# Strassen's form for the values' projection of an attention block, over pairs of token tiles

## The chip, the core and the metric

The kernel runs on one core of a Trainium2 chip. The metric is the device time of one execution in microseconds (us). Engines: PE (TensorE, matmul), ACT (ScalarE), DVE (VectorE), POOL (GpSimd) and SP (SyncE, which here only issues DMAs).

## The reference

Everything is float32. S = 2048 tokens, D = 640 channels, H = 32 heads of 20 channels.

```python
g = sigmoid((x * gate_w).sum(-1, keepdims=True))
qkv = (x @ wqkv).reshape(B, S, 3, H, Dh).transpose(2, 0, 3, 1, 4)
q, k, v = qkv[0], qkv[1], qkv[2]
o = softmax(q @ k.T * Dh ** -0.5) @ v               # per head
a = o.transpose(0, 2, 1, 3).reshape(B, S, D) @ wo
u = gelu(einsum("bsd,sf->bdf", layernorm(x), w1) + b1)   # mixer: over the tokens
b = transpose(einsum("bdf,fs->bds", u, w2) + b2)
return g * a + (1 - g) * b
```

## The kernel before

A float32 product is made of three float32r products. Every operand is split into a high and a low part (`hi_lo`: ACT copies the high part, DVE or POOL subtracts for the low part), and `mm3` adds high·high, high·low and low·high in one PSUM bank.

The stages follow each other on PE: the first two of ten 128-column blocks of q and k (16 units of `qk_unit`, each 15 matmuls of 512 columns, to 63 us), the values (called V here, 63 to 134 us), the other 24 units of q and k (to 216 us), the mixer's two products (to about 720 us) with part of a score pass between them, the attention loop, and the output product. PE, ACT and DVE run in the order in which the code is written (`manual_schedule`); POOL and SP are ordered by the tile scheduler up to the end of V and by hand after it.

A unit's PSUM bank is one of four in turn (`one_tile`: s3, pv, one0, one1). After its matmuls ACT writes the high part (`evh`, three buffers), DVE the low part (`evl`, two buffers), and SP stores both to DRAM. For the second block of k every second unit also stores a difference of two units: DVE copies or subtracts (`kf`), ACT takes the high part (`dh`), DVE the low part in place, and POOL issues four stores (`kd_d`). A buffer is written again only after the store that reads it has landed.

V goes over two column halves (`half`, the first with two more columns, the gate's weights and ones) and 16 token tiles of 128. A tile is 15 matmuls: five channel blocks, three products each, with the x tile as weights and 322 or 320 columns of `wv` moving. ACT copies a tile into `vt` (two ACTIVATEs of 160 columns, L469), SP stores it to `v_d`. The two extra columns go to `gs`, and after the first half one DVE instruction makes `negm` (minus the mean of x). In the second half ACT has one more instruction for each tile: the square of x minus its mean, summed into `ssq` (`stats_unit`, tile `xn`, L444). The next stage's weights `w[2]` are split four tiles before V ends.

Of the kernel before, what the change touches and what calls it, by code (L numbers as in the profile page):

```python
# [31 lines left out]
def gated_mix(ctx, tc, xT, x, wqk, wv0, wv1, wo, w1, w1t, b1, w2, b2, out):  # L32
# [6 lines left out]
    def hi_lo(hi, lo, src, hi_eng=None, lo_eng=None):  # L39
        if hi_eng is nc.scalar:  # L40
            nc.scalar.activation(hi, src, AF.Copy)  # L41
        else:
            (hi_eng or nc.vector).tensor_copy(hi, src)
        (lo_eng or nc.vector).tensor_sub(lo, src, hi.bitcast(F32))  # L44
# [6 lines left out]
    def mm3(ps, pairs, between=lambda i: None):  # L51
        n = len(pairs)
        for i, (ah, al, bh, bl) in enumerate(pairs):
            for k, (a, b) in enumerate(((ah, bh), (ah, bl), (al, bh))):
                nc.tensor.matmul(ps, a, b, start=(i == 0 and k == 0), stop=(i == n - 1 and k == 2))  # L55
            between(i)
# [256 lines left out]
    def qk_unit(m, w, q):  # L313
        wh, wl = w
        ps = one_tile([P, 512], f"qk{m}_{q}")
        mm3(ps, [(wh[:, c], wl[:, c], xh[c][q], xl[c][q]) for c in range(NC)], *([keep_warm] if m == q == 0 else []))
# [24 lines left out]
        nc.vector.tensor_sub(kd, kd, ps)  # L341
# [6 lines left out]
        put(kd_d[0, rows, cols], dh.bitcast(F32))
        put(kd_d[1, rows, cols], kd)
# [61 lines left out]
    wvs = [[[pvp.tile([P, HALF + 2 * (1 - half)], F32R, name=f"wv{i}{half}_{c}") for c in range(NC)]
            for i in range(2)] for half in range(2)]
    wv_raw = {}

    def load_wv(half, c):
        n = HALF + 2 * (1 - half)
        raw = pvp.tile([P, HALF + 2], F32, tag="wvr", bufs=5, name=f"wvr{half}_{c}")
        nc.sync.dma_start(raw[:, :n], (wv1 if half else wv0)[:, c])
        wv_raw[half, c] = raw[:, :n]

    def split_wv(half, c):
        hi_lo(wvs[half][0][c], wvs[half][1][c], wv_raw.pop((half, c)), hi_eng=nc.scalar)

    for c in range(NC):
        load_wv(0, c)
    for n in range(8):
        if 2 <= n < 2 + NC:
            split_wv(0, n - 2)
            load_wv(1, n - 2)
# [4 lines left out]
    nc.gpsimd.dma_start(b2_t, b2)
    xjs = {}

    def stats_load(t):
        if t < NT:
            xjs[t] = pvp.tile([P, D], F32, tag="xn", bufs=4, name=f"xn{t}")
            nc.gpsimd.dma_start(xjs[t], x[t * P:(t + 1) * P, :])  # L440

    def stats_unit(t):
        c = slice(t, t + 1)
        nc.scalar.activation(xjs[t], xjs[t], AF.Square, bias=negm[:, c], accum_out=ssq[:, c])  # L444

    for half in range(2):
        wvh, wvl = wvs[half]
        width = HALF + 2 if half == 0 else HALF
        for t in range(NT):
            n = NT * half + t  # L450
            if n == NT - 2:
                for i in range(4):
                    stats_load(i)
            if n == NT:
                nc.vector.tensor_scalar_mul(negm, gs[:, :, 1], -1.0 / D)
            if n in (2, 4, 6, 8, 10):
                split_wv(1, n // 2 - 1)
            if n == 2 * NT - 8:
                raws[2] = w_dma(2)
            if n == 2 * NT - 4:  # L460
                w[2] = load_w(2, raws[2])
# [3 lines left out]
            vt = pvp.tile([P, 8, NPAIR], F32, tag="vt", bufs=3, name=f"vt{half}_{t}")  # L465
            nc.gpsimd.memset(vt[:, :, VW: 32], 0.0)
            for j in range(2):
                nc.gpsimd.memset(vt[:, :, 32 * j + DH], 1.0)
                nc.scalar.activation(vt[:, :, 32 * j: 32 * j + DH], ps[:, :HALF].rearrange("p (h j w) -> p h j w", j=2, w=DH)[:, :, j], AF.Copy)  # L469
            nc.sync.dma_start(v_d[half, t], vt.rearrange("p h w -> p (h w)"))  # L470
            if half == 0:
                nc.vector.tensor_copy(gs[:, t], ps[:, HALF:])
# [90 lines left out]
    for n, (m, q) in enumerate(units):  # L563
        if n % 4 < 2 and n // 4 * 4 + 4 < len(units):
            m2 = units[n // 4 * 4 + 4][0]
            if n % 4 == 0:
                raws[m2] = w_dma(m2)
            else:
                w[m2] = load_w(m2, raws[m2])
        if n == 8:  # L570
# [10 lines left out]
        last_stores = qk_unit(m, w[m], q)  # L581
# [675 lines left out]
```

## Time and profile before

| | us |
|---|---|
| median of three runs | 1765.78 (1764.94 to 1765.88) |
| profiled execution | 1765.93 |
| its span, first to last instruction | 1764.1 |
| q and k, first 16 units | to 63.06 |
| V | 63.06 to 133.9 |
| q and k, other 24 units | to 216.1 |

The span is 1.83 us shorter than the profiled execution's time. In the rows of the profile, "x480" is a count of instructions, a time in brackets is how long the engine sat idle before the row, and "<-" in the brackets names what ended that. A matmul's row of 0.3 us is the time until its result is out; the next matmul starts earlier, so the pace is read from the starts.

### The profile page before, as it was taken

To read this page: it belongs to the slowest core of one execution; us is meant where nothing else is said; L and a number is where in the kernel's file an instruction comes from. 1 tells how busy PE (TensorE), PEld (TensorE's weight loads), DVE (VectorE), ACT (ScalarE), POOL (GpSimd) and SP (SyncE) were. 2 spreads that over 40 slices of the span, in tenths; PEclk is the share of its full clock that TensorE was granted. 3 is DMA by queue.
4 is the path that set the end of the run, shared out by engine and by line. 5 is a ranking of instruction groups with operands and counts; after the bars stand their busy time and mean duration, and the time that the engine had idled before them with its cause. 6 is when DMAs were issued, how large, how long until landed. Compare 5 with 4: busy or idle time off the path is not lost.

```text
span 1764.1 us, 39591 instructions
## 1 busy us (share of the span) xinstructions
PE 1757.8 (100%) x15020; PEld 1089.8 (62%) x15020; DVE 1223.2 (69%) x2377; ACT 1481.9 (84%) x2565; POOL 665.5 (38%) x990
## 2 busy tenths in 40 slices
PE   9999999999999999999999999999999999999999
PEld 7998899999999999533333333333333333333379
DVE  6303289989999889776777676776777677767335
ACT  5354388888888886799999999999999999999941
POOL 1223577789877777211211111121322122111420
PEclk9999999999999999999999999999999999999999
DMA  8767876567675564334314224043263143301444
GB/s 304 248 194 252 268 182 172 143 179 206 181 191 147 164 177 145 88 78 113 65 28 94 55 60 98 19 98 83 43 147 65 33 102 76 73 20 45 141 155 173
DMA packets 156529, 225.20 MB, mean 128 GB/s; under 512 B 66620, under 2 KB 93644, under 8 KB 152912
## 3 DMA queue, kind: packets, MB, share of 16 engines
q1 hardware_dynamic: 137550, 192.81, 39.8%
q0 software_dynamic: 15568, 23.95, 5.8%
q10 hardware_dynamic: 3220, 5.90, 1.1%
q8 instruction: 118, 1.93, 0.5%
q14 instruction: 73, 0.60, 0.1%
HBM read 166.88 MB, written 55.36 MB: 126 GB/s over the span
## 4 chain that ended last, share of the span: by engine, by line
PE 99%; DMA 1%; ACT 0%; DVE 0%; issue 0%; SPq 0%; ACTq 0%; DVEq 0%
PE pv L936 29%; PE st L1035 22%; PE s L213 12%; PE y L49 10%; PE u L49 10%; PE qk L55 8%; PE v L55 4%; PE a L1155 1%; PE a_one L1155 1%; PE a_s L1155 1%; PE a_pv L1155 1%; DMA k_d<-evh 0%; DMA xr<-in_xT_dram 0%; PE a L49 0%; DVE mx L219 0%; PE y L765 0%
## 5 line engine op out<-in xcount | busy, mean ns | idle before, releaser
L219 DVE TENSOR_REDUCE mx<-s 128x1 f32<-128x512 f32 x1280 | 834.7, 686 | 283.1 <-PE s L213 154.6
L1053 ACT ACTIVATE p<-st 128x512 f32<-128x512 f32 x1022 | 561.1, 614 | 0.0
L936 PE MATMUL pv<-p,v 128*32 128x512 f32 x4088 | 544.6, 605 | 0.0
L1042 ACT ACTIVATE p<-st 128x1024 f32<-128x1024 f32 x511 | 530.0, 1037 | 1.2 <-PE st L1035 1.1
L1035 PEld LDWEIGHTS st<-qs_True,ks_True 62*128 62x128 f32 x2044 | 243.9, 185 | 432.6 <-ACT p L1042 426.8
L1035 PE MATMUL st<-qs_True,ks_True 62*128 62x512 f32 x2044 | 494.2, 445 | 0.0
L213 PE MATMUL s<-ks_False,qs_False 60*128 60x512 f32 x1152 | 322.5, 391 | 0.4 <-ACT p L1053 0.2
L44 POOL TENSOR_TENSOR wl<-wr,wh 128x512 fp32r<-128x512 f32 x228 | 275.2, 1218 | 62.4 <-ACT wh L41 42.7
L238 DVE CUSTOM_DVE_ANT_0 ov<-s,ov 128x512 f32<-128x512 f32 x384 | 263.7, 687 | 36.4 <-PE s L213 26.0
L228 ACT ACTIVATE ov<-s 128x512 f32<-128x512 f32 x384 | 228.6, 597 | 63.1 <-PE s L213 56.6
L213 PE MATMUL s<-sk,sq 60*128 60x512 f32 x896 | 281.3, 394 | 0.0
L917 POOL DMA_DIRECT2D l_d<-oev x124 | 60.4, 494 | 380.5 <-DVE oev L909 376.8
L49 PE MATMUL y<-gh,wh 64*128 64x320 f32 x896 | 198.8, 305 | 0.0
L936 PEld LDWEIGHTS pv<-p,v 128*32 128x32 f32 x4088 | 80.5, 108 | 186.9 <-issue 175.2
L213 PEld LDWEIGHTS s<-ks_False,qs_False 60*128 60x128 f32 x1152 | 192.6, 184 | 3.4 <-ACT p L1053 0.7
L49 PE MATMUL y<-gh,wl 64*128 64x320 f32 x832 | 192.2, 305 | 0.0
L49 PE MATMUL y<-gl,wh 64*128 64x320 f32 x832 | 192.2, 305 | 0.0
L49 PE MATMUL u<-hh,wh 64*128 64x320 f32 x864 | 189.3, 304 | 0.0
L49 PE MATMUL u<-hl,wh 64*128 64x320 f32 x864 | 189.2, 304 | 0.0
L41 ACT ACTIVATE wh<-wr 128x512 fp32r<-128x512 f32 (+3 forms) x247 | 146.9, 599 | 37.9 <-PE y L49 15.0
L49 PE MATMUL u<-hh,wl 64*128 64x320 f32 x800 | 177.8, 304 | 0.0
L213 PEld LDWEIGHTS s<-sk,sq 60*128 60x128 f32 x896 | 166.3, 186 | 15.0
(189 smaller groups left out, 2385.2 us busy)
## 6 DMA issues: line engine op xcount, KB each, us to landing
wr<-in_w_dram SPq DMA_DIRECT2D x192, 256.0 KB
ks_True<-k_d SPq DMA_DIRECT2D x96, 160.0 KB
qs_True<-q_d SPq DMA_DIRECT2D x192, 80.0 KB
qs_False<-q_d SPq DMA_DIRECT2D x96, 80.0 KB
v_d<-vt SPq DMA_DIRECT2D x32, 212.0 KB
sk<-k_d SPq DMA_DIRECT2D x42, 160.0 KB
sq<-q_d SPq DMA_DIRECT2D x84, 80.0 KB
v<-v_d SPq DMA_DIRECT2D x15, 424.0 KB
```

What stands on the lines that cost most here:

```text
L41: nc.scalar.activation(hi, src, AF.Copy)
L44: (lo_eng or nc.vector).tensor_sub(lo, src, hi.bitcast(F32))
L49: nc.tensor.matmul(ps[k], a[r], b[r], start=start, stop=stop)
L55: nc.tensor.matmul(ps, a, b, start=(i == 0 and k == 0), stop=(i == n - 1 and k == 2))
L213: nc.tensor.matmul(ps, qs[half][r, t * P:(t + 1) * P], ks[r, kc * 512:(kc + 1) * 512], start=True, stop=True)
L219: nc.vector.tensor_reduce(mx[:, slot, j, t: t + 1], ps, axis=AX.X, op=OP.max)
L228: nc.scalar.activation(over[j, kc], ps, AF.Relu)
L238: nc.vector.tensor_tensor_reduce(ov, ps, ov, 1.0, -3.0e38, OP.add, OP.max, mx[:, slot, j, t: t + 1])
L936: nc.tensor.matmul(pv[r: r + 32, :], v_tiles[p][:, kt, VW * j: VW * j + 32], pt[j, c], start=(kt == 0), stop=(kt == NT - 1))
L1035: nc.tensor.matmul(ps, ks[r, kt * P:(kt + 1) * P], qs[qh][r, c * 512:(c + 1) * 512], start=True, stop=True)
L1042: nc.scalar.activation(pt, ps, AF.Exp, scale=SCALE)
L1053: nc.scalar.activation(pt, ps, AF.Exp, scale=SCALE)
```

## The change

V is done for two token tiles (t0 even, t1 odd), both column halves and channel blocks 0 to 3 at a time, as a 2x2 product in Winograd's form of Strassen's algorithm: seven products in place of eight. Channel block 4 stays a plain product. With A11, A12 the first column half's weights (blocks 0-1 and 2-3) and A21, A22 the second half's, and x11, x12 (blocks 0-1) and x21, x22 (blocks 2-3) the transposed x of tiles t0 and t1:

- S1 = A21+A22, S2 = S1-A11, S3 = A11-A21, S4 = A12-S2 are made once, by DVE, between the second eight units, and split (`wvh`, `wvl`, widths 644 and 966 columns in place of 320). Their raw loads now stand ahead of the second eight units.
- T1 = x12-x11, T2 = x22-T1, T3 = x22-x12, T4 = x21-T2 are made by POOL for each pair (four subtractions of 256 columns, `vr`) from a 512 KB load of x (`vx`, SP) and split by ACT and DVE (`vT`, 1024 columns).
- A pair has three banks. X takes x·A11 (the head, 6 matmuls), then T2·S2 (6), T3·S3 (6) and T4·A22 with block 4 (9). Y takes x·A12 with block 4 (9, the head). Z takes T1·S1 with block 4 (9) and, after it is read, x·S4 with block 4 (9). ACT copies X to SBUF after each of its first three steps (`sn_0`, `sn_1`, `sn_2`), and DVE adds such a copy to Y or Z on the way to `vt` (two instructions of 160 columns and one of 2 for `gs`).
- PE's order in round i: head of pair i (X 6, Y 9); tail of pair i-1 (X 9, Z 9); body of pair i (T2·S2 6, Z 9, T3·S3 6).
- `negm` is made for two tiles in each tail, and the two `xn` instructions follow there, so the statistics run through all of V. The `xn`, `vx` and `vr` tiles share six buffers of `q4`; `vT` and the later `dh` and `kf` of the second k block share three of `k8`.
- The first unit of the next stage, `qk_unit(2, w[2], 0)`, stands between the last body and the last tail.

```diff
-    for half in range(2):
...
-            ps = one_tile([P, width], f"v{half}_{t}")
-            q, cols = t // 4, slice((t % 4) * P, (t % 4 + 1) * P)
-            mm3(ps, [(xh[c][q][:, cols], xl[c][q][:, cols], wvh[c], wvl[c]) for c in range(NC)])
...
+    def v_sums(i):
...
+        nc.gpsimd.tensor_sub(t[T1], r12, r11)
+        nc.gpsimd.tensor_sub(t[T2], r22, t[T1])
+        nc.gpsimd.tensor_sub(t[T3], r22, r12)
+        nc.gpsimd.tensor_sub(t[T4], r21, t[T2])
+    def v_split(i):
+        t = v_ts[i] = k8([P, 2, 8, P], F32R, f"vT{i}")
+        hi_lo(t[:, 0], t[:, 1], v_rs.pop(i), hi_eng=nc.scalar)
...
+    v_split(0)
...
+    def v_head(i):
+        t0 = 2 * i
+        v_ps[i] = [v_bank(i, k) for k in range(3)]
+        X, Y, Z = v_ps[i]
+        v_mm(X, [(v_x(t0, k), v_w(A11, k)) for k in range(2)], True)
+        v_mm(Y, [(v_x(t0, 2 + k), v_w(A12, k)) for k in range(2)] + [(v_x(t0, 4), v_w(7, 0))], True)
+        a = v_snap(i, 0)
+        if i + 1 < NT // 2:
+            v_split(i + 1)
+        v_out(0, t0, Y, a)
+    def v_body(i):
...
+        v_mm(X, [(v_t(i, T2, k), v_w(S2, k)) for k in range(2)], False)
+        b = v_snap(i, 1)
+        v_mm(Z, [(v_t(i, T1, k), v_w(S1, k)) for k in range(2)] + [(v_x(t1, 4), v_w(7, 1))], True)
+        v_mm(X, [(v_t(i, T3, k), v_w(S3, k)) for k in range(2)], False)
+        c = v_snap(i, 2)
+        v_out(1, t1, Z, c)
+        v_sn[i] = b
+    def v_tail(i):
...
+        v_mm(X, [(v_t(i, T4, k), v_w(A22, k)) for k in range(2)] + [(v_x(t0, 4), v_w(7, 1))], False)
+        v_mm(Z, [(v_x(t1, 2 + k), v_w(S4, k)) for k in range(2)] + [(v_x(t1, 4), v_w(7, 2))], False)
+        v_ts.pop(i)
+        v_out(1, t0, X)
+        v_out(0, t1, Z, v_sn.pop(i))
+        c = slice(t0, t0 + 2)
+        nc.vector.tensor_scalar_mul(negm[:, c], gs[:, c, 1], -1.0 / D)
+        for t in (t0, t1):
+            stats_unit(t)
+    for i in range(NT // 2):
+        if i + 1 < NT // 2:
+            v_sums(i + 1)
+        if i + 2 < NT // 2:
+            v_load(i + 2)
+        v_head(i)
+        if i:
+            v_tail(i - 1)
+        for t in (2 * i, 2 * i + 1):
+            stats_load(t)
+        v_body(i)
...
+        if i == NT // 2 - 1:
+            w[2] = load_w(2, raws[2])
+    qk_unit(2, w[2], 0)
+    v_tail(NT // 2 - 1)
```

The first place is V's start on ACT. Before, the last unit's `evh` and `dh` are followed by the copies of V's tiles:

```order
L41 ACTIVATE evh_3_702<-qk_3_686 128x512
L41 ACTIVATE dh_3_711<-kf_2_684 128x512
L469 ACTIVATE vt_0_734<-v_0_718 128x8x20 x2
L469 ACTIVATE vt_1_758<-v_1_742 128x8x20 x2
L41 ACTIVATE wv_0_476<-wvr_0_546 128x320
```

Now they are followed by the first pair's T (`vT_723`), the copy of X after the head, the second pair's T (`vT_755`), and the copies of X that the body's matmuls wait for:

```order
L41 ACTIVATE evh_3_709<-qk_3_693 128x512
L41 ACTIVATE dh_3_718<-kf_2_689 128x512
L41 ACTIVATE vT_723<-vr_576 128x1024
L525 ACTIVATE sn_0_753<-v_0_735 128x322
L41 ACTIVATE vT_755<-vr_728 128x1024
L525 ACTIVATE sn_1_776<-v_0_735 128x322
L525 ACTIVATE sn_2_793<-v_0_735 128x322
```

`vT_723` and both copies stand behind `dh`, and `vT_755` lies in the buffer of `dh_3_718`, so it waits until the store of that tile has landed.

That store is POOL's. Before, the four stores of the last unit follow each other there:

```order
L338 DMA kd_d<-evh_3_702 128x512
L339 DMA kd_d<-evl_3_703 128x512
L348 DMA kd_d<-dh_3_711 128x512
L349 DMA kd_d<-kf_2_684 128x512
L466 MEMSET vt_3_808 128x8x11
```

Now two subtractions of the third pair stand between them:

```order
L342 DMA kd_d<-evh_3_709 128x512
L343 DMA kd_d<-evl_3_710 128x512
L449 TENSOR_TENSOR vr_802<-vx_733 128x256
L451 TENSOR_TENSOR vr_802<-vx_733 128x256
L354 DMA kd_d<-dh_3_718 128x512
L355 DMA kd_d<-kf_2_689 128x512
L450 TENSOR_TENSOR vr_802<-vx_733,vr_802 128x256
L452 TENSOR_TENSOR vr_802<-vx_733,vr_802 128x256
```

The store of `dh` moved behind them.

The second place is a round on ACT. Before, a tile's copy and one `xn` take turns in the second half:

```order
L469 ACTIVATE vt_0_1137<-v_0_1121 128x8x20 x2
L444 ACTIVATE xn_1064,ssq<-xn_1064,negm 128x640
L469 ACTIVATE vt_1_1163<-v_1_1147 128x8x20 x2
L444 ACTIVATE xn_1066,ssq<-xn_1066,negm 128x640
L469 ACTIVATE vt_2_1189<-v_2_1173 128x8x20 x2
```

Now, for pair 2 (banks `v_0_919` to `v_2_921`) and the tail of pair 1 (`v_0_809`):

```order
L525 ACTIVATE sn_0_937<-v_0_919 128x322
L41 ACTIVATE vT_939<-vr_912 128x1024
L536 ACTIVATE vt_2_968<-v_0_809 128x8x20 x2
L497 ACTIVATE xn_876,ssq<-xn_876,negm 128x640
L497 ACTIVATE xn_878,ssq<-xn_878,negm 128x640
L525 ACTIVATE sn_1_996<-v_0_919 128x322
L525 ACTIVATE sn_2_1013<-v_0_919 128x322
```

The tail's two `xn`, which wait for `negm` and so for the tail's last result, stand ahead of `sn_1`, and PE's T3·S3 of the same round waits for `sn_1`.

The third place is V's end on ACT. Before, the split of the next stage's weights (`wh_1435`) has four tiles behind it:

```order
L444 ACTIVATE xn_1327,ssq<-xn_1327,negm 128x640
L41 ACTIVATE wh_1435<-wr_1329 128x640
L469 ACTIVATE vt_12_1455<-v_12_1439 128x8x20 x2
L444 ACTIVATE xn_1355,ssq<-xn_1355,negm 128x640
L469 ACTIVATE vt_13_1479<-v_13_1463 128x8x20 x2
```

Now it stands behind the last body's `sn_2`, and the unit that needs it is PE's next work:

```order
L525 ACTIVATE sn_1_1536<-v_0_1462 128x322
L525 ACTIVATE sn_2_1553<-v_0_1462 128x322
L41 ACTIVATE wh_1562<-wr_1352 128x640
L41 ACTIVATE evh_0_1582<-qk_0_1566 128x512
L536 ACTIVATE vt_14_1606<-v_0_1462 128x8x20 x2
```

The split moved from ahead of V's last four tiles to right ahead of its use. Behind V, from the first load of the mixer's x on, every engine's instructions stand in the same order as before.

More of the change, by code (lines that the diff above doesn't have):

```diff
@@ L332, in qk_unit @@
         if q % 2 == 0:
-            pool, tag = (p1, "kf") if q == 0 or c == 2 else (pvp if c else px, "kf2")
-            k_first[c] = pool.tile([P, 512], F32, tag=tag, bufs=1, name=f"kf{c}_{q}")
+            if q == 0 or c == 2:
+                k_first[c] = p1.tile([P, 512], F32, tag="kf", bufs=1, name=f"kf{c}_{q}")
+            elif c:
+                k_first[c] = k8([P, 512], F32, f"kf{c}_{q}")
+            else:
+                k_first[c] = px.tile([P, 512], F32, tag="kf2", bufs=1, name=f"kf{c}_{q}")
             nc.vector.tensor_copy(k_first[c], ps)
@@ L343, in qk_unit @@
             dh = p1.tile([P, 512], F32R, tag="evh", bufs=3, name=f"dh{c}_{q}")
+        elif c:
+            dh = k8([P, 512], F32R, f"dh{c}_{q}")
         else:
-            dh = (pvp if c else px).tile([P, 512], F32R, tag="dh", bufs=1, name=f"dh{c}_{q}")
+            dh = px.tile([P, 512], F32R, tag="dh", bufs=1, name=f"dh{c}_{q}")
         hi_lo(dh, kd.bitcast(F32R), kd, hi_eng=nc.scalar)
@@ L409, in gated_mix @@
     pvp = pvs.enter_context(tc.tile_pool(name="pvp", bufs=1, side="right"))
[L411 to L425, printed above, removed]
-    for n in range(8):
-        if 2 <= n < 2 + NC:
-            split_wv(0, n - 2)
-            load_wv(1, n - 2)
+    W = HALF + 2
+    A11, A12, A22, S1, S2, S3, S4 = range(7)
+    T1, T2, T3, T4 = range(4)
+    wvh = [pvp.tile([P, 2, W], F32R, name=f"wvh{i}") for i in range(7)] + [pvp.tile([P, 3, W], F32R, name="wvhc")]
+    wvl = [pvp.tile([P, 2, W], F32R, name=f"wvl{i}") for i in range(7)] + [pvp.tile([P, 3, W], F32R, name="wvlc")]
@@ new lines, in gated_mix, with load_wv, split_wv @@
+    wr = [k8([P, 6, W], F32, f"wvr{i}") for i in range(2)]
+    r11, r21, r22 = (wr[0][:, 2 * i: 2 * i + 2] for i in range(3))
+    r12, rc = wr[1][:, :2], wr[1][:, 2:5]
+    def load_wv(dst, src, cs):
+        nc.sync.dma_start(dst[:, :, :src.shape[2]], src[:, cs])
+        if src.shape[2] < W:
+            nc.gpsimd.memset(dst[:, :, HALF:], 0.0)
+    def split_wv(i, raw):
+        hi_lo(wvh[i], wvl[i], raw, hi_eng=nc.scalar)
+    for dst, src, cs in ((r11, wv0, slice(0, 2)), (r21, wv1, slice(0, 2)), (r22, wv1, slice(2, 4)),
+                         (r12, wv0, slice(2, 4)), (rc[:, :1], wv0, slice(4, 5)), (rc[:, 1:2], wv1, slice(4, 5))):
+        load_wv(dst, src, cs)
@@ new lines, in gated_mix, with v_load @@
+    v_xs, v_rs, v_ts = {}, {}, {}
+    def v_load(i):
+        v_xs[i] = q4([P, 4, 2 * P], F32, f"vx{i}")
+        nc.sync.dma_start(v_xs[i], xT[:4 * P, 2 * P * i: 2 * P * (i + 1)].rearrange("(c p) s -> p c s", p=P))
+    def v_sums(i):
+        r = v_xs.pop(i)
+        r11, r12, r21, r22 = (r[:, 2 * k: 2 * k + 2, n * P:(n + 1) * P] for k in range(2) for n in range(2))
+        v_rs[i] = q4([P, 8, P], F32, f"vr{i}")
+        t = [v_rs[i][:, 2 * j: 2 * j + 2] for j in range(4)]
+        nc.gpsimd.tensor_sub(t[T1], r12, r11)
+        nc.gpsimd.tensor_sub(t[T2], r22, t[T1])
+        nc.gpsimd.tensor_sub(t[T3], r22, r12)
+        nc.gpsimd.tensor_sub(t[T4], r21, t[T2])
@@ new lines, in v_split @@
+    def v_split(i):
+        t = v_ts[i] = k8([P, 2, 8, P], F32R, f"vT{i}")
+        hi_lo(t[:, 0], t[:, 1], v_rs.pop(i), hi_eng=nc.scalar)
+    for n in range(8):
+        if n == 1:
+            split_wv(A11, r11)
+            split_wv(A12, r12)
+        if n == 2:
+            split_wv(A22, r22)
+            nc.vector.tensor_add(r22, r22, r21)
+            nc.vector.tensor_sub(r21, r11, r21)
+            v_load(0)
+        if n == 3:
+            split_wv(S1, r22)
+            nc.vector.tensor_sub(r22, r22, r11)
+            v_sums(0)
+        if n == 4:
+            nc.vector.tensor_sub(rc[:, 2:], rc[:, :1], rc[:, 1:2])
+            split_wv(7, rc)
+            v_load(1)
+        if n == 5:
+            split_wv(S2, r22)
+            nc.vector.tensor_sub(r12, r12, r22)
+        if n == 6:
+            split_wv(S3, r21)
+        if n == 7:
+            split_wv(S4, r12)
@@ L438, in stats_load @@
         if t < NT:
-            xjs[t] = pvp.tile([P, D], F32, tag="xn", bufs=4, name=f"xn{t}")
+            xjs[t] = q4([P, D], F32, f"xn{t}")
             nc.gpsimd.dma_start(xjs[t], x[t * P:(t + 1) * P, :])
@@ L444, in stats_unit @@
         nc.scalar.activation(xjs[t], xjs[t], AF.Square, bias=negm[:, c], accum_out=ssq[:, c])
-    for half in range(2):
[L447 to L461, printed above, removed]
-            ps = one_tile([P, width], f"v{half}_{t}")
-            q, cols = t // 4, slice((t % 4) * P, (t % 4 + 1) * P)
-            mm3(ps, [(xh[c][q][:, cols], xl[c][q][:, cols], wvh[c], wvl[c]) for c in range(NC)])
[L465 to L472, printed above, removed]
-            else:
-                stats_unit(t)
-                stats_load(t + 4)
@@ new lines, in v_mm, with v_x, v_w @@
+    def v_mm(ps, pairs, start):
+        for i, (a, b) in enumerate(pairs):
+            for k, (h, l) in enumerate(((0, 0), (0, 1), (1, 0))):
+                nc.tensor.matmul(ps, a[h], b[l], start=start and i == k == 0,
+                                 stop=i == len(pairs) - 1 and k == 2, skip_group_check=not start)
+    def v_x(t, c):
+        cols = slice((t % 4) * P, (t % 4 + 1) * P)
+        return xh[c][t // 4][:, cols], xl[c][t // 4][:, cols]
+    def v_w(i, k):
+        return wvh[i][:, k], wvl[i][:, k]
@@ new lines, in v_t, with v_bank, v_snap @@
+    def v_t(i, j, k):
+        return v_ts[i][:, 0, 2 * j + k], v_ts[i][:, 1, 2 * j + k]
+    v_ps = {}
+    def v_bank(i, k):
+        if i % 2 and k:
+            return s_tile([P, W], f"v{i}_{k}")
+        tag = "one1" if k == 0 and i % 2 else ("s3", "pv", "one0")[k]
+        return psum.tile([P, W], F32, tag=tag, bufs=1, name=f"v{i}_{k}")
+    def v_snap(i, k):
+        sn = pvp.tile([P, W], F32, tag="sn", bufs=6, name=f"sn{i}_{k}")
+        nc.scalar.activation(sn, v_ps[i][0], AF.Copy)
+        return sn
@@ new lines, in v_out @@
+    def v_out(half, t, ps, add=None):
+        vt = pvp.tile([P, 8, NPAIR], F32, tag="vt", bufs=3, name=f"vt{half}_{t}")
+        nc.gpsimd.memset(vt[:, :, VW: 32], 0.0)
+        for j in range(2):
+            nc.gpsimd.memset(vt[:, :, 32 * j + DH], 1.0)
+            dst = vt[:, :, 32 * j: 32 * j + DH]
+            src, other = (e[:, :HALF].rearrange("p (h j w) -> p h j w", j=2, w=DH)[:, :, j] if e is not None else None for e in (ps, add))
+            if add is None:
+                nc.scalar.activation(dst, src, AF.Copy)
+            else:
+                nc.vector.tensor_add(dst, src, other)
+        if half == 0:
+            nc.vector.tensor_add(gs[:, t], ps[:, HALF:], add[:, HALF:])
+        nc.sync.dma_start(v_d[half, t], vt.rearrange("p h w -> p (h w)"))
@@ new lines, in gated_mix @@
+    v_sn = {}
+    def v_head(i):
[9 more added lines that the diff above has]
+    def v_body(i):
+        t1 = 2 * i + 1
+        X, Y, Z = v_ps[i]
+        v_mm(X, [(v_t(i, T2, k), v_w(S2, k)) for k in range(2)], False)
[5 more added lines that the diff above has]
+        v_sn[i] = b
@@ L580, in gated_mix @@
             w_raw(1)
-        last_stores = qk_unit(m, w[m], q)
+        if n:
+            last_stores = qk_unit(m, w[m], q)
         if n == 23:
```

4 lines of the change are left out of this document (added).

## The prediction

> **What bounds the kernel now.** I read the chain of waits first, then PE's own waits, then V's stretch engine by engine.
>
> ```profile
> span 1764.1 us, 39591 instructions
> PE 99%; DMA 1%; ACT 0%; DVE 0%; issue 0%; SPq 0%; ACTq 0%; DVEq 0%
> ...
> PE warm_ps L372 <- DVE warm L369: 1.4, 1, 1.4
> PE qk L55 <- ACT wh L41: 0.4, 1, 0.4
> PE s L213 <- ACT p L1053: 0.2, 1, 0.2
> PE qk L55 <- DVE xl L44: 0.2, 1, 0.2
> ...
> 10.34 52.89 PE qk L55 x231
> 63.22 70.86 PE v L55 x480
> 134.08 78.99 PE qk L55 x345
> ```
>
> The chain is PE almost throughout, PE waits 2.2 us in all (nearly all before 9 us), and V is one unbroken piece of 480 matmuls. So each matmul removed from V is time gained, and each wait put into V is time lost, unless a later stage gives it back.
>
> **Matmuls.** A pair of tiles took 60 matmuls and takes 54 (seven products of two blocks, six matmuls each, and four times three for block 4): 432 in place of 480, all of 322 columns.
>
> ```profile
> 63.06 0.46 PE L55 MATMUL v<-wv,xh 128*128 128x322 f32 x2
> ...
> 98.70 0.47 PE L55 MATMUL v<-wv,xh 128*128 128x320 f32 x2
> ```
>
> The first half's 240 matmuls take 98.70 - 63.06 = 35.64 us, 148.5 ns each. 432 of them are 64.15 us against 70.86: **6.7 us less**. A round of 54 is 8.02 us.
>
> **What is added, and what hides it.** Per pair ACT gets three copies of X and a T split, POOL four subtractions, DVE a T split and the additions for three of four outputs. Per round ACT is busy some 4.8 us, DVE 3.3, POOL 5 (four subtractions of 0.74, the memsets, two DMA issues), so none of them is full in 8 us. Per round the DMAs carry four `v_d` of 212 KB, two `xn` of 320 KB and one `vx` of 512 KB, 2.05 MB, 223 to 256 GB/s in a round of 9.2 to 8.0 us, about what V's second half carries now:
>
> ```profile
> 30.00:45.00 15.00, 15.00 (x68) 12.29 (x67) 6.50 (x10) 3.65 (x6) 3.46 (x15) 1.00 0.74 253
> 45.00:75.00 30.00, 30.00 (x161) 26.75 (x160) 11.13 (x23) 9.04 (x23) 6.04 (x14) 1.00 0.96 311
> ...
> 100.00:134.00 34.00, 34.00 (x234) 34.00 (x233) 0.82 (x1) 20.43 (x61) 9.95 (x53) 1.00 0.74 228
> ```
>
> (PE, PEld, DVE, ACT, POOL busy, granted clock, DMA share, GB/s.) So what the additions cost in busy time I set at nothing; what they cost lies in the order, at three places where PE waits.
>
> **The wait in each round.** PE's T3·S3 waits for `sn_1`, which ACT reaches only after the tail's two `xn`; these wait for `negm`, the last link behind the tail's Z. Between the tail's last matmul and T3·S3 stand 15 matmuls, 2.23 us of cover. The chain against it, from these rows:
>
> ```profile
> 101.25 0.50 ACT L469 ACTIVATE vt<-v 128x160 f32<-128x160 f32 x2 [1.71 <-PE v L55]
> 125.83 0.83 ACT L444 ACTIVATE xn<-xn,negm 128x640 f32<-128x640 f32 x1
> 126.55 0.20 ACT L444 ACTIVATION_READ_ACCUMULATOR xn<-xn,negm 128x1 f32 x1
> 126.65 0.73 ACT L41 ACTIVATE wh<-wr 128x640 fp32r<-128x640 f32 x1
> ...
> 70.50 0.49 DVE L44 TENSOR_TENSOR wv<-wvr,wv 128x320 fp32r<-128x320 f32 x1 [0.19 <-ACT wv L41]
> 99.57 0.16 DVE L472 COPY gs<-v 128x2 f32<-128x2 f32 x1 [2.07 <-ACT vt L469]
> 99.77 0.17 DVE L455 TENSOR_SCALAR negm<-gs 128x16 f32<-128x16 f32 x1
> 127.41 0.82 DVE L44 TENSOR_TENSOR wl<-wr,wh 128x640 fp32r<-128x640 f32 x1 [27.47 <-ACT wh L41]
> ...
> 60.91 0.46 ACT L41 ACTIVATE wv<-wvr 128x322 fp32r<-128x322 f32 x1
> ...
> 7.20 0.61 ACT L41 ACTIVATE wh<-wr 128x512 fp32r<-128x512 f32 x1
> ...
> 7.87 0.50 PE L55 MATMUL qk<-xh,wh 128*128 128x512 f32 x1 [0.45 <-ACT wh L41]
> ```
>
> - PE to its reader: 0.35 us. The first tile of the second half ends its issue at 98.70 + 15 x 0.1467 = 100.90, ACT starts at 101.25. I use it for DVE too.
> - DVE: no row has an addition of 160 columns. Between 2 columns (0.16) and 320 (0.49) it is 0.32, with 0.08 of overlap 0.24 each; then `gs` 0.2 (99.57 to 99.77) and `negm` 0.17: 0.85.
> - ACT: 0.05 to start, two `xn` at 0.82 from one start to the next (125.83 to 126.65), `sn_1` 0.46: 2.15.
> - PE restarts 0.06 later (7.87 after 7.20 + 0.61).
>
> Sum 3.41, less 2.23 of cover: **1.18 us in each of rounds 1 to 7, 8.2 us**. With additions at 0.16 or at 0.49 it is 0.85 or 1.5 a round, 6 to 10.5 us. The other waits are covered: `sn_0` and the T split are ACT's first work in a round and needed 4 us later; `sn_2` has the next head behind it (2.2 us for 0.8); `vr` is done a round ahead.
>
> **The wait at V's start.** Before, V began behind four free banks, so PE did not feel that the evacuation of the last unit was late:
>
> ```profile
> 63.31 0.60 ACT L41 ACTIVATE evh<-qk 128x512 fp32r<-128x512 f32 x1 [1.45 <-PE qk L55]
> 68.70 0.63 ACT L41 ACTIVATE dh<-kf 128x512 fp32r<-128x512 f32 x1 [4.80 <-DVE kf L341]
> 69.24 0.87 ACT L469 ACTIVATE vt<-v 128x160 f32<-128x160 f32 x4
> ...
> 67.33 0.69 DVE L44 TENSOR_TENSOR evl<-qk,evh 128x512 fp32r<-128x512 f32 x1 [3.05 <-DMA k_d<-evl]
> 67.94 0.68 DVE L341 TENSOR_TENSOR kf<-kf,qk 128x512 f32<-128x512 f32 x1
> ...
> 61.30 0.54 POOL L348 DMA_DIRECT2D kd_d<-dh  x1 [0.72 <-ACT dh L41]
> ...
> DMA to landing us min/median/max: 3.0/4.9/6.6
> ```
>
> (The last line is that of the `kd_d` stores.) `dh` started 5.6 us after PE had left the unit, because `evl` waited for a store of two units earlier, in the full DMA stretch above. Now PE has only the head's 15 matmuls (2.23 us, to 65.29) before it needs `sn_0` and `vT_723`, both behind that `dh` on ACT.
>
> How late will `evl` be? 1.64 MB of `wv` loads leave the stretch from 43.6 us on and so do 1.31 MB of `xn`; three `vx` (1.57 MB) and one `xn` (0.33) come. The stretch 30 to 45 has 26% of its DMA time free, about 1.2 MB, for the `wv` loads and the first `vx` (2.16 MB), so 0.95 spills over. That leaves 0.95 + 1.05 + 0.33 = 2.33 MB for 2.95: 2 us earlier at 311 GB/s. DVE also gets 6.9 us of weight splits and 3.8 of sums between the units in place of 2.5, which would be covered by its waits there. So `evl` at 65.3, `kf` 65.9, `dh` 66.65, `vT_723` 67.2 to 68.25, its low part on DVE (1.22 by the 320- and 640-column rows) to 69.5. PE's third matmul of T2·S2, due at 65.6, starts at 69.5.
>
> Then POOL: the store of `evl` to 66.6, two subtractions of 0.74, the store of `dh` at 68.3, landed 4.9 later at 73.2. `vT_755` waits for that, and `sn_1` stands behind it:
>
> ```profile
> L1042 ACT ACTIVATE p<-st 128x1024 f32<-128x1024 f32 x511 | 530.0, 1037 | 1.2 <-PE st L1035 1.1
> ...
> L44 POOL TENSOR_TENSOR wl<-wr,wh 128x256 fp32r<-128x256 f32 x32 | 23.7, 740 | 9.0 <-ACT wh L41 5.2 <-PE s L213 3.0 <-DMA wr<-in_w_dram 0.4
> ```
>
> 73.2 + 0.94 + 0.46 + 0.06: T3·S3 at 74.7. It was due after 30 matmuls, at 67.5. **7.2 us at the start**, both waits together. With `evl` free at once (63.95) and a landing in 3.0 it is 4.0; with `evl` as late as before and a landing in 6.6 it is 10.9.
>
> **The wait at V's end.** The unit moved ahead of the last tail needs `w[2]`, whose split now follows `sn_2` of the last body: 0.35, `sn_2` 0.36 to the next start, high part 0.73, DVE 0.04 + 0.82, PE 0.06 make 2.36 until the third matmul, less two matmuls of 0.23: **1.9 us** (1.6 to 2.2). The unit's own 3.43 us only change place, and the statistics' tail with the three table loads then has three units of q and k as cover, not four; `wh` of the block after needs 9.1 us of the 10.3.
>
> **Sum.** -6.7 + 7.2 + 8.2 + 1.9 = +10.6 us, on the profiled execution's 1765.93: 1776.5. The median of the runs stands 0.15 lower, so I say 1776.4. All lower ends together give +4.8, all upper ones +16.9.
>
> **Rivals.**
> - *The clock falls in the waits* (17%). The two waits at the start are 3.9 and some 3.3 us long. At the kernel's own start a matmul of 512 columns takes 0.43 us, later 0.229 (52.89 / 231), though the clock's column shows 1.00 in both (below, and in the rows of V above):
>
> ```profile
> 1.45 4.33 PE L372 MATMUL warm_ps<-warm 128*128 128x512 f32 x10 [1.45 <-DVE warm L369]
> ...
> 3.00:5.00 2.00, 2.00 (x6) 1.54 (x5) 0.00 (x0) 0.15 (x1) 1.29 (x3) 1.00 0.91 278
> ```
>
> If each of these waits brings that state back for as long as the ten matmuls there, it costs 10 x (0.43 - 0.229) = 2 us a time: 1780.4. Against it: no wait of this length is in the trace, so none shows a second fall. [...]
> - *The start costs little* (12%): stores land in 3 us, and DVE's `evl` isn't held: 1773.3, still slower.
> - *The delay is given back later* (5% faster, and 6% no change). One stage would have to be paced by something that V's end doesn't move, in the mixer at 216 to 720 us, where DVE is busiest. All 17.3 us given back would make 1759.2; it decides from 10.6 us upwards. Against it: PE issues evenly there,
>
> ```profile
> 300.00:400.00 100.00, 100.00 (x1245) 99.69 (x1245) 90.47 (x231) 84.87 (x170) 83.06 (x91) 1.00 0.60 165
> 400.00:500.00 100.00, 100.00 (x1247) 100.00 (x1246) 90.35 (x228) 84.49 (x170) 86.55 (x99) 1.00 0.72 192
> ```
>
> 1245 and 1247 matmuls in 100 us, and nothing of that stage starts before V is over.
>
> **Numbers.** My forecast, slower by 7 to 14 us, has 60%; the clock rival 17%, the cheap start 12%, faster 5%, no change 6%. About 0.2%, 3.5 us, is what a measurement here can tell from no change: slower 89%, same 6%, faster 5%. The range goes from 1770.5, near the sum of the lower ends, to 1782.5, near that of the upper ones and beyond the clock rival.
>
> **What would show it.** V's stretch on the chain, from the first v matmul to the end of the last tail and the moved unit, at 85 us (70.86 + 3.43 + 10.6). PE rows of v with idle time ahead: one of about 1.2 us in each of seven rounds, released by ACT `sn`; two of 3 to 4 us between 65 and 75, released by DVE `vT` and ACT `sn`; one or two before the moved unit, by ACT and DVE `wh`, `wl`. A round of 9.2 us. I am wrong if the rounds come at 8.0 (then the chain through `xn` is shorter than I add it), if `vT_755` doesn't wait for a store, or if the total moves less than V.

## The result and the profile after

The changed kernel takes 1789.96 us (median of four runs, 1789.76 to 1790.4), the kernel before 1765.49 in the same session: 1.0139 times as long, interval 1.0122 to 1.0157. It is slower, as forecast, but by 24.5 us and not by 10.6, and above the range (1770.5 to 1782.5). The profiled execution took 1789.76 us.

First the page's head and chain shares of the kernel after, with its list of PE's waits (us in total, times, longest):

```profile
span 1787.9 us, 39575 instructions
PE 93%; issue 2%; DMA 2%; ACT 1%; DVE 1%; POOL 1%; SPq 0%; DVEq 0%; ACTq 0%; POOLq 0%
...
PE v L502 <- ACT sn L525: 20.1, 9, 9.4
...
PE qk L55 <- ACT wh L41: 1.2, 1, 1.2
PE v L502 <- DVE vT L44: 0.5, 1, 0.5
...
PE v L502 <- DVE kf L345: 0.2, 1, 0.2
```

Two rows of its chain (start, us) answer to the last ones shown of before:

```profile
161.61 78.98 PE qk L55 x345
240.59 2.54 PE u L49 x31
```

The 345 matmuls of q and k behind V take 78.98 us. Before, 360 followed V, because the unit of 15 that now stands ahead of the last tail was among them, and the row from 134.08 us on shows the first 345 of them, 78.99 us: the pace is the same. They start 27.5 us later, of which 3.43 are the moved unit, so V costs 24.1 us more. The mixer's first product starts at 240.5 us, before at 216.4, and the span is 23.8 longer. Almost nothing is given back later, so the loss lies in V. These are some of PE's rows there that had idle time ahead (start, us, idle time and its releaser):

```profile
74.93 0.64 PE L502 MATMUL v<-wvh,vT 128*128 128x322 f32 x1 [9.39 <-ACT sn L525]
76.31 0.91 PE L502 MATMUL v<-wvh,vT 128*128 128x322 f32 x2 [0.48 <-DVE vT L44]
81.53 0.42 PE L502 MATMUL v<-wvh,vT 128*128 128x322 f32 x1 [2.00 <-ACT sn L525]
92.15 0.42 PE L502 MATMUL v<-wvh,vT 128*128 128x322 f32 x1 [0.80 <-ACT sn L525]
...
110.83 0.42 PE L502 MATMUL v<-wvh,vT 128*128 128x322 f32 x1 [1.29 <-ACT sn L525]
121.89 0.42 PE L502 MATMUL v<-wvh,vT 128*128 128x322 f32 x1 [2.79 <-ACT sn L525]
...
153.57 0.68 PE L55 MATMUL qk<-xh,wh 128*128 128x512 f32 x1 [1.21 <-ACT wh L41]
```

The waits at the start sum to 12.06 us (0.19, 9.39, 0.48, 2.00), the seven of the rounds to 8.73 (0.80, 0.85, 1.29, 2.79, 1.25, 0.90, 0.85), the last is 1.21: 22.0 us. From the start of V's first matmul to that of its last, without the moved unit, there are 95.1 us (62.73 to 161.30, less 3.43). The 431 steps between them at the pace of 322 columns before (35.64 / 240) are 64.0, so 9.1 us are lost beside the waits, most of them to slower matmuls. Two of PE's rows show the pace:

```profile
82.91 0.47 PE L502 MATMUL v<-wvh,xh 128*128 128x322 f32 x1
83.18 0.47 PE L502 MATMUL v<-wvl,xh 128*128 128x322 f32 x1
```

And three windows of 1 us show the clock (columns as in the windows of before):

```profile
82.00:83.00 1.00, 1.00 (x6) 1.00 (x5) 0.94 (x4) 0.00 (x0) 0.29 (x1) 0.52 0.00 0
83.00:84.00 1.00, 1.00 (x6) 1.00 (x5) 0.38 (x2) 0.44 (x1) 0.25 (x1) 0.50 0.27 100
123.00:124.00 1.00, 1.00 (x6) 1.00 (x5) 0.32 (x2) 0.44 (x1) 0.00 (x0) 0.50 0.86 233
```

Starts are 0.27 us apart in place of 0.148, and the granted clock (third number from the right) is 0.5. By the starts of the matmuls the clock fell four times, at 68.4, 82.0, 123.0 and 153.7 us, and came back at 78.6, 85.5, 126.4 and 157.1. The distances from one of these changes to the next are 3, 1, 11, 1, 8 and 1 times 3.413 us, so all of them lie on one grid of windows of this length. The first fall lasts three windows, and PE works almost only in the last of them. By my estimate from these starts a window at half pace costs 3.41 x (1 - 0.148 / 0.27) = 1.5 us, four of them 6 us. The rest, 3.1 us over 12 waits, comes to an estimated 0.26 us around each wait beside the idle time that the profile gives.

### The profile page after: what moved, and what is told of

Read it like the earlier page. It is cut to its first block, busy times and chain, and to the rows that moved or that the text cites. A ratio compares the mean times of both kernels' runs of the same rounds, so it can differ in the third digit from the quotient of the medians.

```text
span 1787.9 us, 39575 instructions
## 1 busy us (share of the span) xinstructions
PE 1760.3 (98%) x14972; PEld 1088.5 (61%) x14972; DVE 1252.4 (70%) x2443; ACT 1488.6 (83%) x2547; POOL 690.7 (39%) x1025
## 4 chain that ended last, share of the span: by engine, by line
PE 93%; issue 2%; DMA 2%; ACT 1%; DVE 1%; POOL 1%; SPq 0%; DVEq 0%; ACTq 0%; POOLq 0%
PE pv L1058 28%; PE st L1157 22%; PE s L213 12%; PE y L49 10%; PE u L49 9%; PE qk L55 5%; PE v L502 2%; PE a L1277 1%; PE a_one L1277 1%; PE a_pv L1277 1%; PE a_s L1277 1%; ACT xn L497 0%; DMA v_d<-vt 0%; DMA kd_d<-dh 0%; DMA k_d<-evl 0%
```

## The experiments

Three sizes were disputed: what holds `evl` and `dh` at the start, whether the rounds' wait is the link over `xn`, and how much the clock takes. Nothing of the computation is left out in any of these kernels; a time in brackets is the median.

**A third `evl` buffer** (1787.82 us).

```diff
-        tag, bufs = ... else ("evl", 2)
+        tag, bufs = ... else ("evl", 3)
```

> Against the changed kernel (1789.96 us). evl has three buffers in place of two. Theory (the last unit's evl waits for a kd_d store that POOL issued late, and that sets V's start): evl starts when DVE is free, at 67.9 in place of 71.6, dh, vT and sn_0 follow 3.7 us earlier, PE's first wait is 5.7 in place of 9.4, the second (for the store of dh) stays near 2: 1786 us. Rival (the DMA stretch or the vr subtractions set the start): the wait stays at 9 or more, 1789 to 1790.

```profile
65.00 0.68 DVE L44 TENSOR_TENSOR evl<-qk,evh 128x512 fp32r<-128x512 f32 x1
...
69.80 0.63 ACT L41 ACTIVATE dh<-kf 128x512 fp32r<-128x512 f32 x1 [5.92 <-DMA kd_d<-dh]
...
71.76 0.64 PE L502 MATMUL v<-wvh,vT 128*128 128x322 f32 x1 [6.96 <-ACT sn L525]
```

`evl` moved from 71.61 to 65.00, where the prediction had put it, but `dh` came only 3.2 us earlier: its own buffer was still being stored. So the late `evl` was the store's doing, and behind it stood a second buffer that the sum had not looked at. Part of the 6.6 us came from further ahead: with a third buffer the `evl` of two units earlier started 2.9 us earlier too (59.70 in place of 62.56). The first wait fell by 2.4 us.

**Dummy matmuls in the first two waits** (1790.19 us): 50 matmuls ahead of T2·S2 and 8 ahead of T3·S3 of round 0 are added, nothing else.

> Against the changed kernel (1789.96 us). In round 0 alone PE gets 50 matmuls of 322 columns into an unused bank between head and body (7.4 us at full clock) and 8 ahead of T3*S3 (1.2 us); nothing else moves. Theory (the clock falls because PE is idle): PE is busy through most of both waits, the granted clock stays 1.00 to 90 us, the body's 21 matmuls and the next head's run at 0.149 in place of 0.27: 3.3 us less, 1786.7. Rival (the waits' length alone counts, the slow matmuls are a consequence of something else, such as the operands' arrival): 1790 or, with the extra matmuls in the way, 1791.

```profile
73.69 0.41 PE L502 MATMUL v<-wvh,vT 128*128 128x322 f32 x1 [1.29 <-ACT sn L525]
...
81.03 0.41 PE L502 MATMUL v<-wvh,vT 128*128 128x322 f32 x1 [1.50 <-ACT sn L525]
...
110.14 0.63 PE L502 MATMUL v<-wvh,vT 128*128 128x322 f32 x1 [2.33 <-ACT sn L525]
```

By the matmuls' starts the clock now fell once at the start (75.7 to 79.1) in place of twice, and V took 2.5 us less in the profiled execution (1788.19 us), the fastest of the four. Later it fell at 109.9, behind a wait of 2.33 us in a round where it had not fallen, in place of 123.0, and at V's end as in the changed kernel (150.8). With 3.2 us of waits at the start in place of 12.06 the clock was down there for one window in place of four; as a cure the dummies are worth nothing, since the median stayed where it was.

**The changed kernel once more**, for the clock (1793.20 us, one execution). The expectation on record was that the falls would come at other places, three or five of them, and that each fall more or less would move 1790 us by 1.6. PE's waits in V sum to 27.0 us in place of 22.0. By the matmuls' starts the clock fell three times in place of four, at 68.7, 82.4 and 157.5 us (mean granted clock 0.995, in the first trace 0.994). Two waits of 2.78 and 3.13 us in rounds had no fall behind them; each lay in two windows of the grid (1.85 and 0.94, 1.63 and 1.49). 5.0 us more of waits and one window less at half pace make 3.5; the execution was 3.4 us longer. The number of falls went as expected (the one in the rounds is gone, those at the start and the end stay), the time did not, because the waits themselves differ between executions.

**Four units as cover.** Units 0 to 3 of block 2 of q, which otherwise follow V, go ahead of V; a unit of the block after takes their place behind the last body (1784.32 us).

> Against the changed kernel (1789.96 us). The four units qk(2, 0..3) stand ahead of V in place of behind it (13.7 us of PE work that needs nothing of V's preparation), and the weights of the unit that stands ahead of the last tail, now qk(7, 0), are split one round earlier. Theory (V's start is late work, not too much work): the waits of 9.4, 0.5 and 2.0 us and the two falls of the clock behind them (3.3) go, at the end 1.2 and a fall (1.7) go, the rounds' waits stay: 1772 us. Rival (the delay is moved, not covered: the mixer has 20 units as cover for its first loads and splits in place of 24): what V gains comes back as waits in the first product of the mixer, 1780 or more.

V's start still has waits of 1.12, 1.82 and 1.86 us, because `evh` and `vT` are held by stores as before, and the rounds sum to 10.1. Cover of 13.7 us removes 7 of the 12 us: the late buffers move with the units. Behind V a new wait of 1.90 us came, with a fall of the clock behind it (183.9 to 187.3).

**Statistics out of the chain.** The two `xn` of a tail are issued after `sn_2`:

```diff
-        for t in (t0, t1):
-            stats_unit(t)        # end of v_tail(i)
+            v_stats(i - 1)       # behind v_body(i)
```

> Against the changed kernel (1789.96 us). The two xn of a tail stand behind the body's sn_1 and sn_2 on ACT. Theory (xn hold sn_1): the seven waits ahead of T3*S3, 8.7 us idle and about 0.26 of restart each (1.8), go; with them the clock's fall behind the 2.79 us wait (1.6) and, since the round's wait no longer adds to the one at V's end in one stretch of 3.4 us, that one too (1.7): 1776 us, no idle row of v by sn_1 between 90 and 150. Rival (the three buffers of vt and the v_d stores pace the round, xn only stands in front): at most a third of it goes, 1786.

It ran in 1782.61 us. The rounds' waits fell from 8.73 to 1.55 us plus 0.48, so the link over `xn` is what made them; what is left waits for a `vt` buffer. But the wait at the end grew from 1.21 to 2.84 us, since the split of `w[2]` now stood behind two `xn`.

**The same with `vx` behind the round's stores on SP and `w[2]` split a round earlier** (1778.28 us):

> Against the changed kernel (1789.96 us) and the first move of xn (1782.61). ACT reads a tail's X (vt) ahead of sn_1, as in the changed kernel, so that the bank is free for the head two pairs on; only the two xn stand behind sn_2. In addition the load vx is written behind the stores of its round, and w[2] is split one round earlier. Theory (ACT's xn and SP's vx held sn_1, the split held the end): no idle row of v behind the start, one fall of the clock or two, all at the start: 1775 us. Rival (three vt buffers and the stores' landing pace the round): waits of 0.5 to 1 us in some rounds stay, 1779 to 1782.

```profile
75.17 0.64 PE L502 MATMUL v<-wvh,vT 128*128 128x322 f32 x1 [9.63 <-ACT sn L525]
80.89 0.64 PE L502 MATMUL v<-wvh,vT 128*128 128x322 f32 x1 [0.93 <-ACT sn L525]
...
129.82 0.41 PE L502 MATMUL v<-wvh,xh 128*128 128x322 f32 x1 [1.82 <-DVE vt L538]
```

Rounds and end together now wait 2.2 us in place of 9.9, the clock falls only at the start (where it stays down from 67.6 to 84.6 us), and the kernel gains 11.7 us on the change. What it still loses is the start.

**The whole reading of a tail's X and Z, and the T split, behind `sn_2`**, with `vx` and `w[2]` as in the last kernel (1786.68 us). X's bank was then read so late that the next round's head waited for it six times, as in this row of V's last round:

> Against the changed kernel (1789.96 us). PE's order is the same. On ACT the reading of a tail (vt, negm's readers xn) and the T split of the next pair stand behind the body's sn_1 and sn_2; the load vx of pair i+2 is written behind the stores of its round, since it waits for a buffer that xn frees and SP held v_d behind it; w[2] is split one round before its use. Theory (two queues hold sn_1: ACT's own xn, and SP, whose vx holds the v_d stores that free vt): all seven round waits go (8.7 idle, 1.8 of restarts) and the wait at the end (1.2), with two falls of the clock (3.1); V's start stays as it is: 1775 us, no idle row of v behind 90 us. Rival (the stores themselves are too slow for three vt buffers): some waits of 0.5 to 1 us stay, 1779 to 1782.

```profile
140.82 0.42 PE L502 MATMUL v<-wvh,xh 128*128 128x322 f32 x1 [1.93 <-ACT vt L536]
```

**Start and rounds together** took several steps: PE gets units of the next block as cover ahead of V (two in e_both, then one), the last one's reading waits until after V's first body, `dh` gets a buffer of its own, and T of the first pair is split three units earlier. e_both has the rounds of e_round (1788.65 us), e_all those of e_stats2 (1783.56). In e_all2 (1777.78) the last k unit too is read behind the first body, SP stores its difference, the T split stands behind `sn_2`, the second unit goes ahead of the last tail, and `vt` has four buffers. In e_all3 (1776.25) POOL issues the `vx` loads from the third pair on:

> Against the kernel before (1765.8 us). As the one above, and V's start: T of pair 0 is split two units earlier, dh of the second k block has a buffer of its own, its last one is made behind the first body, two of the four units qk(2, q) stand ahead of V as cover (6.9 us of PE work that V does not wait for), and the last one's evacuation stands behind the first body. Theory (every lost microsecond is a wait or a fall of the clock behind one): no idle row of v, granted clock 1.00 throughout, V 64.2 us and the moved unit, 1759 us. Rival 1 (the DMA stretch ahead of V holds evl and so DVE, whatever the order): 2 to 5 us of waits stay at the start, 1762 to 1766. Rival 2 (the cover is missing behind V): waits in the k units that follow V, 1762 or more.

> Against the kernel before (1765.5 us). The one above with V's start mended: T of pair 0 split two units earlier, a buffer of its own for dh of the second k block, the last of them made behind the first body, unit qk(2, 0) as cover ahead of V and qk(2, 1) between the first body and the second head, and the raw weights of block 7 loaded earlier. Theory (each lost microsecond is a wait or a fall of the clock behind one, and none is left): V's stretch is 64.2 us and three units of 3.43, granted clock 1.00 throughout, stage behind V as before: 1759 us, 0.4% under the kernel before. Rival (the DMA stretch ahead of V or the shorter cover behind V holds PE once more): one or two waits of 2 to 5 us with a fall of the clock, 1763 to 1768.

> Against the kernel before (1765.6 us) and the first attempt at all of it (1783.56). New: the last k unit is read behind the first body and its difference stored by SP; only qk(2, 0) stands ahead of V; qk(2, 1) stands ahead of the last tail, with block 7's weights split before it; four vt buffers (six sn become four, to make room); the T split of the next pair behind sn_2. Theory (the waits of the first attempt were a T buffer behind a late kf store, 5.9, a bank behind evl, 1.9, vt buffers, 6.5, and block 7's split behind the table loads, 4.6): none is left, V's stretch is 64.2 us and two units, clock 1.00, 1759 us; with one wait of 2 us left and a fall behind it 1763. Rival (the stretch ahead of V carries more bytes than it can, so a wait turns up wherever the next store is needed): 5 us or more of waits and at least one fall, 1767 or more, no better than before.

> Against the second attempt (1777.78 us), whose PE did not wait at V's start at all and then 13.5 us in rounds 2 to 6. One edit: the loads vx from pair 2 on are issued by POOL in place of SP. Theory (SP stands at vx until POOL has read the last one, with the v_d stores behind it; these free vt, on which ACT, DVE and POOL wait, and so sn_1): the waits and the falls behind them go, 1759 to 1763 us, under the kernel before (1765.4). Rival (the stores themselves land too late, or POOL's own queue takes the place of SP's): waits of 1 to 3 us in three or more rounds stay, 1770 or more.

All four missed; for the last two the rival came true. In e_all2 PE doesn't wait from 66.55 to 87 us, so the start was cured, yet four waits of 2.6 to 4.2 us stood in the rounds. Moving `vx` from SP to POOL put them behind POOL's own queue: POOL then waited 4.0 to 5.7 us for each x in three rounds, and T came late:

```profile
94.47 1.06 ACT L41 ACTIVATE vT<-vr 128x1024 fp32r<-128x1024 f32 x1 [5.49 <-POOL vr L465]
```

**The order of POOL and SP written by hand through V, one more `xn` buffer, X's `vt` between `sn_1` and `sn_2`, `vt` with three buffers again** (1768.86 us):

> Against the kernel before (1765.4 us) and the last attempt (1776.25), in whose rounds POOL issued a vx only when the last one was read, so that T came late and ACT with it. Here POOL's and SP's order in V is written by hand too: vx two rounds ahead on SP ahead of the stores, the xn loads at a round's end, a place of its own for every second xn (so that vx finds a free buffer), vt of X between sn_1 and sn_2, three vt buffers. Theory (what is left in the rounds is the order of two queues and the number of buffers, nothing that the arithmetic needs): waits of 2 us or less in all, 1759 to 1763 us, under the kernel before. Rival (with five engines and two DMA queues in one ring a round of 8 us can't be held): rounds of 9 us or more and falls of the clock, 1770 or more.

```profile
88.38 0.64 PE L524 MATMUL v<-wvh,xh 128*128 128x322 f32 x1 [4.68 <-DVE vt L562]
...
87.77 0.56 DVE L562 TENSOR_TENSOR vt<-v,sn 128x160 f32<-128x160 f32 x2 [8.60 <-DMA v_d<-vt]
```

But for one, the rounds now come every 8.0 to 8.7 us, and one wait above 0.5 us is left: three `vt` buffers, and stores that SP issued late.

**A fourth `vt` buffer, its room taken from `dh`'s own** (1763.98 us, eleven runs; ratio 0.9995, interval 0.9986 to 1.0004), **and in a second kernel the `vx` loads and two `kd_d` stores behind the tail's `v_d` on SP** (1778.18 us):

> The last version with a fourth vt buffer, its room taken from the buffer that kept dh apart (dh again shares the three evh buffers). My account: the wait of 4.68 us in round 1 falls to about 1 us, the clock stays up in V, 1762 us (1759 to 1765), below the kernel before. Rival: the form itself costs, since the vt buffers only move the wait to the next buffer or queue: 1767 to 1770 as in the version before.

> The same, and SP's order in round 1 changed: the last two kd stores and each vx load go behind the two v_d stores of the tail. My account: no wait above 0.5 us is left in V, 1760 us (1758 to 1764). Rival: vx then lands too late for POOL's subtractions and the wait comes back in rounds 2 to 5 as PE waiting for ACT vT, 1766 to 1772.

PE's waits with the fourth buffer, the first of them at the kernel's end:

```profile
PE a_s L1315 <- DVE oy L1321: 2.1, 1, 2.1
...
PE v L524 <- DVE gs L564: 1.3, 1, 1.3
PE v L524 <- ACT sn L549: 0.9, 2, 0.5
```

2.16 us of waiting are left in V, and the clock doesn't fall there (mean granted clock of the execution 0.999). V with the moved unit takes 70.5 us (before 70.7 without it). The form's saving is real: the loss was waits and what follows them. The later `vx`, though, made POOL wait 4.2 to 4.5 us a round for x, and ACT's `vt` wait for stores of V: PE waits 10.7 us in V.

With the fourth buffer the mixer starts 3.5 us earlier than in the kernel before (212.9 against 216.4), and 3.7 us are lost again at the end. There POOL issues the last `o_d` stores 3.2 us after their data, which DVE had written by 1693.65, with no release that the profile shows:

```profile
1696.87 2.04 POOL L1080 DMA_DIRECT2D o_d<-oev  x4 [18.93 <-issue]
```

**Eight more memsets on POOL** (1764.85 us) and, beside them, **`vx` behind the tail's stores in round 1 alone** (1763.62 us, eleven runs, before 1765.86 in the same session; ratio 0.9987, interval 0.9978 to 0.9996):

> The version before with eight more memsets of one column on POOL in round 0, nothing else. If POOL's pause of about 2.5 to 3.2 us stands at a fixed count of its instructions, it moves ahead of the wait for the last oev and is hidden: the last o_d stores start 0.3 us behind their copy, PE's wait of 2.11 us at the end and the half clock behind it (1.5 us) are gone, 1760.5 us (1759 to 1762). Rival: the pause hangs on the data or the DMAs and stays where it is: 1764 us.

> The same, and in round 1 alone the vx load goes behind the two v_d stores of the tail on SP. The wait of 1.25 us in round 2 (PE for DVE gs, behind a vt buffer that its store held) goes to about 0.3: 1759.5 us (1758 to 1762). Rival: vx lands too late for POOL's subtractions as when all loads were moved, and a wait of 2 us or more comes in round 2: 1764 to 1768.

```profile
136.15 75.55 PE qk L55 x330
211.70 2.54 PE u L49 x31
```

These are rows of e_all10's chain; PE waits 1.4 us in its V. In e_all9 it waits 1.6, and the mixer starts at the same time (211.6 us in both), so no effect of the later `vx` on V is shown. POOL's pause of 3.2 us stayed ahead of the last `o_d` in both kernels, so the idea of a fixed count fell. Yet e_all10's profiled execution (1760.88 us, the fastest of its eleven) has no wait at the end, while e_all7 and e_all9 wait 2.1 and 1.8 us there: the pause doesn't decide it, and what does stays open. e_all10 is the only one whose interval lies below the kernel before, by 0.13%, less than a measurement here can tell from no change.

## Why the prediction was right or wrong

- *Matmuls, -6.7.* Right as far as the runs show: in e_all10 the mixer's first product starts at 211.7 us, in the kernel before at 216.4. That is 4.7 us of the 6.7, with 1.4 us of waits left in V and some 0.26 around each of them; no version without any wait was run.
- *The start, 7.2.* This is the term that failed first: 12.06 us. The step was "`evl` at 65.3", and with it the work on the weights that DVE was to do "covered by its waits". `evl` started 6.3 us later. Before, the `evl` of two units earlier and its store were these:

```profile
59.05 0.69 DVE L44 TENSOR_TENSOR evl<-qk,evh 128x512 fp32r<-128x512 f32 x1 [0.16 <-DMA q_d<-evl]
...
60.04 0.54 POOL L339 DMA_DIRECT2D kd_d<-evl  x1 [2.02 <-DVE evl L44]
```

  After:

```profile
61.27 1.37 DVE L477 TENSOR_TENSOR wvr<-wvr,wvr 128x644 f32<-128x644 f32 x1
62.56 0.68 DVE L44 TENSOR_TENSOR evl<-qk,evh 128x512 fp32r<-128x512 f32 x1
...
67.11 0.82 DVE L44 TENSOR_TENSOR wvl<-wvr,wvh 128x644 fp32r<-128x644 f32 x1
71.61 0.69 DVE L44 TENSOR_TENSOR evl<-qk,evh 128x512 fp32r<-128x512 f32 x1 [3.68 <-issue]
...
60.62 1.33 POOL L451 TENSOR_TENSOR vr<-vx 128x256 f32<-128x256 f32 x1
...
65.45 0.54 POOL L343 DMA_DIRECT2D kd_d<-evl  x1
...
80.09 1.06 ACT L41 ACTIVATE vT<-vr 128x1024 fp32r<-128x1024 f32 x1 [5.21 <-DMA kd_d<-dh]
```

  I had reasoned with bytes: loads leave the stretch, so stores land earlier. What counted was when the store is issued that frees the buffer: at 65.45, before at 60.04, and `evl` followed 6.2 us behind it. Of these 5.4 us some 3.5 are DVE's: it reached the `evl` of two units earlier at 62.56 in place of 59.05, behind a split and a sum of the weights. The other 1.9 are POOL's queue: ahead of the store stood four subtractions (59.93 to 64.05), which waited for `vx` and of which two ran at 1.33 and 1.32 us in place of 0.74, and two DMA issues. The upper bound of 10.9 us was passed because neither DVE's work on the weights nor POOL's queue ahead of that store was in any of the three cases. The second wait had the chain as written, `vT_755` behind the store of `dh`, then `sn_1`, but took 2.0 us where the sum had 3.3.
- *The rounds, 8.2.* Right in size (8.73) and in cause, as e_stats shows. In detail five of the seven waits are 0.80 to 1.25 us, and the other two (1.29 and 2.79) have a second chain that I hadn't seen, the free `vt` buffer. In round 4:

```profile
116.02 0.50 ACT L536 ACTIVATE vt<-v 128x160 f32<-128x160 f32 x2 [1.70 <-DMA v_d<-vt]
118.75 0.55 DVE L538 TENSOR_TENSOR vt<-v,sn 128x160 f32<-128x160 f32 x2 [2.65 <-DMA v_d<-vt]
119.78 0.83 ACT L497 ACTIVATE xn<-xn,negm 128x640 f32<-128x640 f32 x1 [3.26 <-issue]
...
121.19 0.38 SPq L442 DMA_DIRECT2D vx<-in_xT_dram  x1
121.66 2.95 SPq L541 DMA_DIRECT2D v_d<-vt  x2
```

  Stores of V stand on SP behind a `vx` load that waits for its own buffer.
- *The end, 1.9.* 1.21, with a fall of the clock behind it.
- *The clock rival, 17%.* This was the other failed step. That the clock falls behind waits is right (granted clock 0.50 behind those of 9.39, 2.00 and 2.79 us), its size was not: I gave it 2 us a time and only at the start. It took an estimated 6 us, because falls came after waits of 2.0 and 2.8 us and after two short ones in a row (0.85 and 1.21 us) too. By the rows the cost is 1.5 us a time, and four falls came. The 0.26 us around each wait was in no term.
- *Sum.* -6.7 + 12.06 + 8.73 + 1.21 + 9.1 = +24.4. V began 0.3 us earlier than before (62.73, 63.06), which leaves the 24.1 by which the mixer starts later; the profiled executions differ by 23.8. Of what the forecast lacks, 4.9 us are the start and 9.1 the slow clock and the time around the waits; the rounds add 0.5, and the end takes 0.7 back.
- *Given back later.* Right to be given little: V's delay stays to the last instruction.

## What to carry to other kernels

Before an algorithm with fewer products replaces an engine's unbroken stream, count the buffers and queue places of everything that now stands between two of its products, not only the arithmetic: here 7 us of saving cost 31 us of waits and slow clock until buffers, queue order and bank reads were arranged for it. When a wait depends on a store, follow the queue that issues the store, with what stands ahead of it there, before the bytes. And price every wait of some 2 us on TensorE with the half-speed window that can follow it: here 3.41 us at a granted clock of 0.50, an estimated 1.5 us lost, behind waits of 2.00 and 2.79 us.

## What was not expected of the hardware

- In these traces the clock also fell behind windows in which PE worked. In the windows at full clock, worked out from the matmuls' starts, it fell where one held a single wait of 1.90 us or more (1.90 in e_cover), and in some with two waits of together 1.6 to 1.75 (e_warm); where a window held a single piece of 1.54 to 1.84, as for the six waits of e_round, it didn't. Once down, it stayed down behind windows with shorter waits (0.77 and 0.93 us in e_stats2). So a window little more than half idle (1.90 of 3.413 us) was enough here.
- Some of POOL's and DVE's instructions took longer beside each other. In the changed kernel a subtraction of 256 columns on POOL took 0.74 us at 59.93 and 1.32 to 1.33 while DVE split and summed weights (60.06 to 62.6 us), and DVE's sum of 644 columns took 0.83 us at 54.87, with POOL's subtractions over, and 1.37 beside them. Beside DVE's `kf` (63.16 us) POOL's took 0.73. What makes the difference isn't shown.
- The versions spread more from run to run than the kernel before does (e_stats 1780.6 to 1784.2, the changed kernel 1789.8 to 1793.2 in two sessions, before 1764.9 to 1765.9 in its first four runs, but 1764.5 to 1768.4 in the 21 of the last session). In the two traces of the changed kernel both the waits and the windows that they meet differ. That this is the whole of the spread isn't shown: with 2.2 us of waits in V, the version with a fourth `vt` buffer spread from 1761.6 to 1768.1.
